# Adding the old attention state on TensorE, and updating the state earlier in the even groups

## The chip, the cores and the metric

The kernel runs on one core of a Trainium2 chip. The time is device microseconds (us) of one execution, from an uploaded program to the finished output; of the kernel before, the median of three runs is 358.19 us.

## The reference

Two stages follow each other. The first is a gated linear attention over 4 batches, 8 heads, 768 steps and 48 channels; the second a two-layer network on the 3072 resulting rows, with a rational function between its layers.

```python
f = 1.0 / (1.0 + np.exp(-f_logit))
for t in range(S):
    state = f[:, :, t, :, None] * state + einsum('bhd,bhe->bhde', k[:, :, t], v[:, :, t])
    y[:, :, t] = einsum('bhd,bhde->bhe', q[:, :, t], state)
...
h = x @ w_in                                   # 3072x384 by 384x2048
P = a[0] + a[1]*h + a[2]*h**2 + a[3]*h**3
Q = 1.0 + abs(b[0])*abs(h) + abs(b[1])*h**2
out = (P / (Q + 1e-6)) @ w_out                 # by 2048x384
```

## The kernel before

**Attention.** Time is cut into 6 chunks of 128 steps, the batches into 2 halves; a *unit* is one chunk of one half, so there are 12, numbered ku (chunk ku // 2, half ku % 2). Each half keeps its state in one SBUF tile `state`, 128 x 2 x 4 x 48 in bf16, for 2 batches and 4 head pairs. For a unit, ScalarE (ACT) takes exp and ln of the gates (`a_ef`), TensorE (PE) sums them along time (`a_cs`), ACT takes exp of the sums (`a_exp`: A and Ai), VectorE (DVE) scales q and k by them (`a_mul`), PE transposes the result (`a_T`) and ACT copies it (`a_Te`). PE forms the scores (`a_sc`), DVE masks them (`a_mask`: scm), and PE makes the output y from the old state and from the masked scores (`a_y`). ACT copies y (`a_ye`: ysb), PE transposes it (`a_x`: xps), and ACT copies that into xT (`a_xe`), the input of the network.

**The state.** `a_sv` (L147) puts two things into one PSUM bank `sv`: the column sums of the gates' logarithms (L156, 8 matmuls) and the chunk's increment of the state (L163, 16 matmuls). `a_al` (L213) has ACT turn the sums into the decay `alast`. `a_st` (L220) has DVE compute, in two instructions, stmp = sv + state (L232) and state = stmp * alast (L233); in chunk 0 there is no old state, and one product from `sv` does it (L229). The last chunk needs no update, so units 2 to 9 run the two instructions: eight times.

**One bank for two tiles.** `sv` and `xps` carry the tag w1 of the pool `ps1`, which has one buffer. So the transposes of `a_x` (L240) cannot start before the last reader of `sv` is done. That reader is L232 of the same unit.

**The network.** Its work is cut into 24 groups n: chunk c = n // 4 and a quarter g = n % 4 of the 2048 columns. PE multiplies (`m_h`, two halves into the one buffer `hp`), ACT copies (`m_y`: hy), DVE computes |h| and the denominator (`m_q`: z L280, w L282 and L283), ACT takes ln and exp(-ln) for the reciprocal (`m_ln`: lq L289, `m_ex`: qi L294), DVE computes the numerator (`m_p`: t, L301 to L305) and the product (`m_g`: gall L313). PE multiplies the finished chunk before by w_out (`m_o`, L330), ACT copies (`m_oe`, L340) and the SP queue writes it out.

**Order.** There is no scheduler: each engine runs its instructions in the order in which the program is written. The main loop (L435) takes a pair of groups at a time, p = 0 to 11, an *even* one and an *odd* one, and works the attention of unit ku = p + 3 in between. The even group finishes unit ku - 1 (y's copy, transposes, decay, state) and starts unit ku; the odd one continues unit ku up to y. In the even group the program writes `a_ye`, `m_h`, `a_x`, `a_exp`, `a_al`, `a_xe`, `m_ln`, `m_ex`, `m_p`, `m_o`, `m_y`, `m_h`, `a_mul`, `a_st`, `m_oe`, `a_T`, `m_g`. The eight state updates fall into the even groups of p = 0 to 7.

Loads of q, k and the gates go through the SP queue, those of v through GpSimd's (POOL), three units ahead. In the first 80 us GpSimd also casts the weights to bf16.

Of the kernel before, what the change touches and what calls it, by code (L numbers as in the profile page):

```python
# [8 lines left out]
F32 = mybir.dt.float32  # L9
# [8 lines left out]
def kernel(  # L18
# [12 lines left out]
    nc = tc.nc  # L31
    B, H, S, D = q.shape
    C = 128
    NC = S // C
    P = 128
    HP = H // 2
# [5 lines left out]
    UB = 2  # L42
# [11 lines left out]
    at = ctx.enter_context(tc.tile_pool(name="at", bufs=1))  # L54
# [12 lines left out]
    ident = consts.tile([C, C], BF16, name="ident")  # L67
    mask = consts.tile([C, C], F32, name="mask")
    ones = consts.tile([C, 1], BF16, name="ones")
# [47 lines left out]
    def a_exp(n):  # L117
        s = at_[n]
        s["A"] = at.tile([C, UB, H, D], F32, name="A")
        s["Ai"] = at.tile([C, UB, H, D], F32, name="Ai")  # L120
        for dst, sc in ((s["A"], -1.0), (s["Ai"], 1.0)):
            nc.scalar.activation(dst.rearrange("p b h d -> p b (h d)"), s["cs"][:, :, 0:DM],
                                 AF.Exp, scale=sc)
# [21 lines left out]
        s["qkT"] = t  # L145

    def a_sv(n):  # L147
        s = at_[n]
        if s["c"] == NC - 1:
            return  # L150
        sv = ps1.tile([P, 512], F32, name="sv", tag="w1")
        s["svv"] = sv[:, 0:UB * HP * D].rearrange("p (b h e) -> p b h e", b=UB, h=HP)
        s["al"] = sv[:, 448:448 + UB * HP]
        for j in range(UB):
            for p in range(HP):
                nc.tensor.matmul(s["al"][:, j * HP + p:j * HP + p + 1],  # L156
                                 s["ls"][:, j, 2 * p:2 * p + 2, :].rearrange("t h d -> t (h d)"),
                                 ones, start=True, stop=True)
        for j in range(UB):
            for p in range(HP):  # L160
                for i in range(2):
                    h = 2 * p + i
                    nc.tensor.matmul(s["svv"][64 * i:64 * i + 64, j, p, :],  # L163
                                     s["qk"][:, j, 1, h, :], s["vn"][:, j, h, :],
                                     start=True, stop=True)

    def a_sc(n, j):
        s = at_[n]
# [37 lines left out]
    def a_ye(n):  # L206
        s = at_[n]
        ysb = at.tile([C, UB, DM], BF16, name="ysb")
        nc.scalar.copy(ysb.rearrange("t b (p i e) -> t i (b p) e", p=HP, i=2),
                       s["y"].rearrange("t i b p e -> t i (b p) e"))  # L210
        s["ysb"] = ysb

    def a_al(n):  # L213
        s = at_[n]
        if s["c"] == NC - 1:
            return
        s["alast"] = at.tile([P, UB * HP], F32, name="alast")
        nc.scalar.activation(s["alast"], s["al"], AF.Exp, scale=-1.0)

    def a_st(n):  # L220
        s = at_[n]
        if s["c"] == NC - 1:
            return
        al = s["alast"]
        ab = bass.AP(tensor=al.tensor, offset=al.offset, ap=[al.ap[0], al.ap[1], [0, D]])
        stv = s["st"].rearrange("p b h e -> p (b h) e")
        svf = s["svv"].rearrange("p b h e -> p (b h) e")
        if s["c"] == 0:
            nc.vector.tensor_mul(stv, svf, ab)  # L229
        else:  # L230
            stmp = at.tile([P, UB * HP, D], F32, name="stmp")
            nc.vector.tensor_add(stmp, svf, stv)  # L232
            nc.vector.tensor_mul(stv, stmp, ab)  # L233

    def a_x(n):
        s = at_[n]
        xps = ps1.tile([P, UB, KD, C], BF16, name="xps", tag="w1")
        for j in range(UB):
            for kk in range(KD):
                nc.tensor.transpose(xps[:, j, kk, :], s["ysb"][:, j, kk * P:(kk + 1) * P], ident)  # L240
        s["xps"] = xps

    def a_xe(n):
        s = at_[n]
        c, u = s["c"], s["u"]
        if u == 0:
            xTs[c] = xp.tile([P, KD, B, C], BF16, name="xT")
        nc.scalar.copy(xTs[c][:, :, u * UB:(u + 1) * UB, :].rearrange("p k b t -> p b k t"), s["xps"])  # L248
# [5 lines left out]
    def m_h(n, half):  # L254
        if n >= NGR:
            return
        c, g = divmod(n, NG)
        hp = psh.tile([P, 2, NT], F32, name="hp", tag="h")
        xT = xTs[c].rearrange("p k b t -> p k (b t)")
        for e in range(2):  # L260
            m = g * G + half * 2 + e
            for kk in range(KD):
                nc.tensor.matmul(hp[:, e, :], w_in_sb[:, kk, m * P:(m + 1) * P], xT[:, kk, :],  # L263
                                 start=(kk == 0), stop=(kk == KD - 1))
        mg.setdefault(n, {})["hp", half] = hp

    def m_y(n, half):
        if n >= NGR:
            return
        s = mg[n]  # L270
        if half == 0:
            s["y"] = ms.tile([P, W], BF16, name="hy")
        nc.scalar.copy(s["y"][:, half * 2 * NT:(half + 1) * 2 * NT],  # L273
                       s["hp", half].rearrange("p a n -> p (a n)"))

    def m_q(n):

        s = mg[n]
        z = ms.tile([P, W], BF16, name="z", bufs=1)
        nc.vector.tensor_scalar(z.bitcast(U16), s["y"].bitcast(U16), 0x7FFF, None, op0=ALU.bitwise_and)  # L280
        w = ms.tile([P, W], BF16, name="w", bufs=1)
        nc.vector.tensor_scalar(w, z, babs[:, 1:2], babs[:, 0:1], op0=ALU.mult, op1=ALU.add)  # L282
        nc.vector.tensor_mul(w, w, z)  # L283
        s["w"] = w

    def m_ln(n):
        s = mg[n]
        s["lq"] = ms.tile([P, W], F32, name="lq", bufs=1)
        nc.scalar.activation(s["lq"], s["w"], AF.Ln, bias=one_eps)  # L289

    def m_ex(n):
        s = mg[n]
        s["qi"] = ms.tile([P, W], BF16, name="qi")
        nc.scalar.activation(s["qi"], s["lq"], AF.Exp, scale=-1.0)  # L294

    def m_p(n):

        s = mg[n]
        y = s["y"]
        t = ms.tile([P, W], BF16, name="t")  # L300
        nc.vector.tensor_scalar(t, y, a_sb[:, 3:4], a_sb[:, 2:3], op0=ALU.mult, op1=ALU.add)  # L301
        nc.vector.tensor_mul(t, t, y)  # L302
        nc.vector.tensor_scalar(t, t, a_sb[:, 1:2], None, op0=ALU.add)  # L303
        nc.vector.tensor_mul(t, t, y)  # L304
        nc.vector.tensor_scalar(t, t, a_sb[:, 0:1], None, op0=ALU.add)  # L305
        s["t"] = t
# [75 lines left out]
    a_sc(0, 0)  # L382
    a_sc(0, 1)
    a_sv(0)
    a_exp(1)
    a_mask(0, 0)
# [12 lines left out]
    a_sc(1, 0)  # L399
    a_sc(1, 1)  # L400
    a_sv(1)
    a_ef(2)
    a_mask(1, 0)
# [31 lines left out]
    for p in range(NGR // 2):  # L435
        ku = p + 3
        for odd in range(2):
            n = 2 * p + odd
            c, g = divmod(n, NG)
            last = c == NC - 1  # L440
            has, prev = ku < NUN, ku - 1 < NUN
            m_y(n + 1, 0)
            m_q(n)
            if not odd:
                if prev:
                    a_ye(ku - 1)
                m_h(n + 1, 1)
                if prev:
                    a_x(ku - 1)
                if has:  # L450
                    a_exp(ku)
                if prev:
                    a_al(ku - 1)
                    a_xe(ku - 1)
                m_ln(n)
                m_ex(n)
                m_p(n)
                m_o(c - 1, g)
                m_y(n + 1, 1)
                m_h(n + 2, 0)  # L460
                if has:
                    a_mul(ku)
                if prev:
                    a_st(ku - 1)
                m_oe(c - 1, g)
                if has:
                    a_T(ku)
            else:
                if has:
                    a_Te(ku)  # L470
                m_h(n + 1, 1)
                m_ln(n)
                m_ex(n)
                if has:
                    a_sc(ku, 0)
                    a_sc(ku, 1)
                    a_sv(ku)
                m_p(n)
                m_o(c - 1, g)
                m_y(n + 1, 1)  # L480
                m_h(n + 2, 0)
                if has:
                    a_mask(ku, 0)
                    a_mask(ku, 1)
                if ku + 1 < NUN:
                    a_ef(ku + 1)
                m_oe(c - 1, g)
                if has:
                    a_y(ku)
                if ku + 1 < NUN:  # L490
                    a_cs(ku + 1)
                if ku + 3 < NUN:
                    load(ku + 3)
            m_g(n)
            if last:
                for b in range(B):
                    m_o(c, b, range(g * G, (g + 1) * G))
# [32 lines left out]
```

## Time and profile before

| what | us |
|---|---|
| median of three runs (357.04 to 358.89) | 358.19 |
| the profiled execution, whole | 357.51 |
| its span, first to last instruction | 355.2 |
| busy in the span: DVE | 273.3 |
| busy in the span: ACT | 224.2 |
| busy in the span: PE | 206.3 |
| DVE idle ahead of gall (L313), 24 instances together | 39.8 |

An engine that works all the time would show 355.2 us of busy time. How the engines' idle times hang together is read from the waits and from the order of events in one pair. In the loop's middle a pair takes 27.8 us, from one even z to the next.

### The profile page before, as it was taken

What the parts mean: (1) busy time and instruction counts of PE and PEld (TensorE: products, weight loads), DVE (VectorE), ACT (ScalarE), POOL (GpSimd) and SP (SyncE); (2) the same over time, 40 slices, a digit from 0 to 9 for tenths busy, and PEclk for the clock granted to TensorE, in tenths of its full rate; (3) what the DMA queues carried; (4) which work ended last, traced back from release to release, by engine and by line L of the source; (5) the groups of instructions that cost most, each with busy time, mean ns of one, the idle gap of its engine ahead of it and who ended that gap; (6) DMA issues with size and microseconds to landing.
All of it is one profiled execution on the core that took longest, in us unless ns stands there. A gap on an engine that the chain in (4) does not pass through costs nothing.

```text
span 355.2 us, 4363 instructions
## 1 busy us (share of the span) xinstructions
PE 206.3 (58%) x1722; PEld 113.1 (32%) x1744; DVE 273.3 (77%) x290; ACT 224.2 (63%) x214; POOL 37.0 (10%) x42
## 2 busy tenths in 40 slices
PE   0364730750455881882683584575478575868764
PEld 0153320420223440441351352242244332334431
DVE  3264294998599499499499499499589999999981
ACT  4437545670683892793694586487389776776641
POOL 5032620460001001002002002000000000000000
PEclk9999995886586797697699699699699999699996
DMA  9998999698304009009109208300000000010002
GB/s 142 170 214 209 227 166 173 231 236 96 70 2 22 23 5 173 22 2 155 22 24 137 43 22 111 68 23 24 0 22 24 22 24 22 2 43 24 22 22 89
DMA packets 107315, 27.80 MB, mean 78 GB/s; under 512 B 100640, under 2 KB 105760, under 8 KB 107296
## 3 DMA queue, kind: packets, MB, share of 16 engines
q1 hardware_dynamic: 82336, 25.18, 34.0%
q0 software_dynamic: 24960, 2.36, 12.6%
q8 instruction: 13, 0.21, 0.3%
q14 instruction: 6, 0.05, 0.1%
HBM read 25.17 MB, written 4.72 MB: 84 GB/s over the span
## 4 chain that ended last, share of the span: by engine, by line
DVE 63%; ACT 15%; issue 7%; DMA 7%; PE 5%; SPq 2%; DVEq 0%; ACTq 0%
DVE gall L313 8%; DVE t L302 7%; DVE w L283 7%; DVE t L304 7%; DVE w L282 6%; ACT lq L289 5%; DMA kn<-in_k_dram 5%; DVE t L303 5%; DVE z L280 5%; ACT qi L294 4%; DVE scm L182 4%; DVE t L301 4%; DVE t L305 3%; DVE qkp L128 3%; DVE qkp L127 2%
## 5 line engine op out<-in xcount | busy, mean ns | idle before, releaser
L263 PE MATMUL hp<-xT,w_in_sb 128*128 128x512 bf16 x266 | 76.7, 412 | 53.1 <-ACT hy L273 50.0
L330 PE MATMUL op<-w_out_sb,gall 128*128 128x384 bf16 x384 | 80.1, 371 | 5.6 <-DVE gall L313 5.6
L273 ACT CAST hy<-hp 128x1024 bf16<-128x1024 f32 x48 | 48.1, 1003 | 26.2 <-PE hp L263 26.2
L313 DVE TENSOR_TENSOR gall<-t,qi 128x2048 bf16<-128x2048 bf16 x24 | 29.3, 1222 | 39.8 <-ACT qi L294 39.2
L263 PEld LDWEIGHTS <-w_in_sb 128*128 128x128 bf16 x288 | 29.7, 103 | 90.0 <-issue 68.0
L289 ACT ACTIVATE lq<-w,one_eps 128x2048 f32<-128x2048 bf16 x24 | 48.2, 2009 | 10.5 <-DVE w L283 10.5
L330 PEld LDWEIGHTS <-gall 128*128 128x128 bf16 x384 | 41.3, 111 | 39.6 <-issue 15.0
L248 ACT COPY xT<-xps 128x768 bf16<-128x768 bf16 x12 | 9.6, 803 | 67.2 <-PE xps L240 67.2
L294 ACT ACTIVATE qi<-lq 128x2048 bf16<-128x2048 f32 x24 | 45.8, 1910 | 0.8
L240 PE MATMUL xps<-ident,ysb 128*128 128x128 bf16 x72 | 9.1, 291 | 60.3 <-DVE stmp L232 60.1
L182 DVE TENSOR_TENSOR scm<-sc,mask 128x1024 bf16<-128x1024 f32 x24 | 28.2, 1217 | 16.4 <-PE sc L173 16.4
L97 POOL DMA_DIRECT2D vn<-in_v_dram x24 | 22.2, 930 | 133.9 <-PE y L193 133.1
L302 DVE TENSOR_TENSOR t<-t,hy 128x2048 bf16<-128x2048 bf16 x24 | 30.6, 1273 | 0.8
L304 DVE TENSOR_TENSOR t<-t,hy 128x2048 bf16<-128x2048 bf16 x24 | 29.4, 1226 | 0.8
L283 DVE TENSOR_TENSOR w<-w,z 128x2048 bf16<-128x2048 bf16 x24 | 29.4, 1225 | 0.8
L240 PEld LDWEIGHTS <-ysb 128*128 128x128 bf16 x72 | 7.1, 128 | 64.7 <-issue 62.3
L144 ACT COPY qkT<-tp 128x2048 bf16<-128x2048 bf16 x12 | 22.4, 1869 | 0.1
L282 DVE TENSOR_SCALAR w<-z,babs 128x2048 bf16<-128x2048 bf16 x24 | 20.9, 870 | 0.9
L303 DVE TENSOR_SCALAR t<-t,a_sb 128x2048 bf16<-128x2048 bf16 x24 | 19.3, 803 | 0.8
L136 PE MATMUL tp<-ident,qkp 128*128 128x128 bf16 x192 | 15.0, 237 | 7.8 <-DVE qkp L127 6.0
L301 DVE TENSOR_SCALAR t<-hy,a_sb 128x2048 bf16<-128x2048 bf16 x24 | 19.4, 807 | 0.0
L127 DVE TENSOR_TENSOR qkp<-qn,A 128x768 bf16<-128x768 f32 x12 | 11.4, 952 | 9.9 <-DMA qn<-in_q_dram 8.3
(45 smaller groups left out, 215.6 us busy)
## 6 DMA issues: line engine op xcount, KB each, us to landing
fn<-in_f_logit_dram SPq DMA_DIRECT2D x24, 192.0 KB, 5.4
kn<-in_k_dram SPq DMA_DIRECT2D x24, 192.0 KB, 6.2
qn<-in_q_dram SPq DMA_DIRECT2D x24, 192.0 KB, 4.8
out_dram<-osb SPq DMA_DIRECT2D x24, 192.0 KB, 1.9
wst<-in_moe_w_in_dram SPq DMA_DIRECT2D x4, 768.0 KB, 6.6
wst<-in_moe_w_out_dram SPq DMA_DIRECT2D x4, 768.0 KB, 6.0
vn<-in_v_dram POOLq DMA_DIRECT2D x24, 96.0 KB, 5.8
a_sb<-in_moe_a_dram SPq DMA_DIRECT2D x1, 2.0 KB, 3.9
```

Of the source, the lines that this page charges most:

```text
L182: nc.vector.tensor_mul(m, s["sc", j].rearrange("s i p t -> s (i p) t"), mb)
L263: nc.tensor.matmul(hp[:, e, :], w_in_sb[:, kk, m * P:(m + 1) * P], xT[:, kk, :], start=(kk == 0), stop=(kk == KD - 1))
L273: nc.scalar.copy(s["y"][:, half * 2 * NT:(half + 1) * 2 * NT], s["hp", half].rearrange("p a n -> p (a n)"))
L282: nc.vector.tensor_scalar(w, z, babs[:, 1:2], babs[:, 0:1], op0=ALU.mult, op1=ALU.add)
L283: nc.vector.tensor_mul(w, w, z)
L289: nc.scalar.activation(s["lq"], s["w"], AF.Ln, bias=one_eps)
L294: nc.scalar.activation(s["qi"], s["lq"], AF.Exp, scale=-1.0)
L302: nc.vector.tensor_mul(t, t, y)
L303: nc.vector.tensor_scalar(t, t, a_sb[:, 1:2], None, op0=ALU.add)
L304: nc.vector.tensor_mul(t, t, y)
L313: nc.vector.tensor_mul(galls[c][:, g * G:(g + 1) * G, :].rearrange("p a n -> p (a n)"), s["t"], s["qi"])
L330: nc.tensor.matmul(ops[c, b], galls[c][:, mm, b * C:(b + 1) * C], w_out_sb[:, mm, :], start=(mm == 0), stop=(mm == KF - 1))
```

## The change

`a_sv` now adds the old state on PE: between the column sums and the increment one matmul, with the identity as weights and the state as moving operand, goes into the columns of the increment, and the 16 increment matmuls accumulate on it. Only the first of the column sums starts the bank afresh. `a_st` is then a single product from `sv`, in every chunk. In the even groups `a_al` and `a_st` are written ahead of `a_ye`.

```diff
     def a_sv(n):
...
+        s["svf"] = sv[:, 0:UB * HP * D]
+        svv = s["svf"].rearrange("p (b h e) -> p b h e", b=UB, h=HP)
...
-                                 ones, start=True, stop=True)
+                                 ones, start=(j + p == 0), stop=True, skip_group_check=True)
+        if s["c"] > 0:
+            nc.tensor.matmul(s["svf"], ident, s["st"].rearrange("p b h e -> p (b h e)"),
+                             start=False, stop=True, skip_group_check=True)
...
-                    nc.tensor.matmul(s["svv"][64 * i:64 * i + 64, j, p, :],
+                    nc.tensor.matmul(svv[64 * i:64 * i + 64, j, p, :],
                                      s["qk"][:, j, 1, h, :], s["vn"][:, j, h, :],
-                                     start=True, stop=True)
+                                     start=False, stop=True, skip_group_check=True)
...
     def a_st(n):
...
-        stv = s["st"].rearrange("p b h e -> p (b h) e")
-        svf = s["svv"].rearrange("p b h e -> p (b h) e")
-        if s["c"] == 0:
-            nc.vector.tensor_mul(stv, svf, ab)
-        else:
-            stmp = at.tile([P, UB * HP, D], F32, name="stmp")
-            nc.vector.tensor_add(stmp, svf, stv)
-            nc.vector.tensor_mul(stv, stmp, ab)
+        nc.vector.tensor_mul(s["st"].rearrange("p b h e -> p (b h) e"),
+                             s["svf"].rearrange("p (x e) -> p x e", e=D), ab)
...
             if not odd:
                 if prev:
+                    a_al(ku - 1)
+                    a_st(ku - 1)
                     a_ye(ku - 1)
...
                 if prev:
-                    a_al(ku - 1)
                     a_xe(ku - 1)
...
-                if prev:
-                    a_st(ku - 1)
```

DVE in the even group of one pair, before (in brackets the semaphores that an instruction waits for, by engine):

```order
L282 TENSOR_SCALAR w<-z,babs 128x2048 [waits DVE_49]
L283 TENSOR_TENSOR w<-w,z 128x2048 [waits DVE_49]
L301 TENSOR_SCALAR t<-hy,a_sb 128x2048
L302 TENSOR_TENSOR t<-t,hy 128x2048 [waits DVE_49]
L303 TENSOR_SCALAR t<-t,a_sb 128x2048 [waits DVE_49]
L304 TENSOR_TENSOR t<-t,hy 128x2048 [waits DVE_49]
L305 TENSOR_SCALAR t<-t,a_sb 128x2048 [waits DVE_49]
L127 TENSOR_TENSOR qkp_103<-qn,A 128x2x8x48 [waits DMAHW1_49,DMAHW0_49,Activation_49]
L128 TENSOR_TENSOR qkp_103<-kn,Ai 128x2x8x48 [waits DMAHW7_49,DMAHW6_49,Activation_49]
L232 TENSOR_TENSOR stmp<-sv,state_106 128x384 [waits PE_49,Activation_49]
L233 TENSOR_TENSOR state_106<-stmp,alast 128x384 [waits DVE_49,PE_49]
L313 TENSOR_TENSOR gall<-t,qi 128x2048 [waits Activation_49]
```

The same engine and place now (the line numbers are those of the changed kernel):

```order
L281 TENSOR_SCALAR w<-z,babs 128x2048 [waits DVE_49]
L282 TENSOR_TENSOR w<-w,z 128x2048 [waits DVE_49]
L231 TENSOR_TENSOR state_107<-sv,alast 128x384 [waits PE_49,Activation_49]
L300 TENSOR_SCALAR t<-hy,a_sb 128x2048
L301 TENSOR_TENSOR t<-t,hy 128x2048 [waits DVE_49]
L302 TENSOR_SCALAR t<-t,a_sb 128x2048 [waits DVE_49]
L303 TENSOR_TENSOR t<-t,hy 128x2048 [waits DVE_49]
L304 TENSOR_SCALAR t<-t,a_sb 128x2048 [waits DVE_49]
L127 TENSOR_TENSOR qkp_102<-qn,A 128x2x8x48 [waits DMAHW1_49,DMAHW0_49,Activation_49]
L128 TENSOR_TENSOR qkp_102<-kn,Ai 128x2x8x48 [waits DMAHW7_49,DMAHW6_49,Activation_49]
L312 TENSOR_TENSOR gall<-t,qi 128x2048 [waits DVE_49,Activation_49]
```

The last reader of `sv` stood behind five instructions of the numerator and two of `a_mul`; it stands right behind w now, and the addition is gone.

ACT in the same group, before (from the copy of the next group's h to the reciprocal):

```order
L273 CAST hy<-hp 128x1024 [waits DVE_49,PE_49]
L209 CAST ysb<-y 128x2x8x48 [waits PE_49]
L122 ACTIVATE A<-cs 128x768 [waits PE_49]
L122 ACTIVATE Ai<-cs 128x768
L218 ACTIVATE alast<-sv 128x8
L248 COPY xT<-xps 128x2x3x128 [waits PE_49]
L289 ACTIVATE lq<-w,one_eps 128x2048 [waits DVE_49]
```

And now:

```order
L272 CAST hy<-hp 128x1024 [waits DVE_49,PE_49]
L223 ACTIVATE alast<-sv 128x8
L214 CAST ysb<-y 128x2x8x48 [waits PE_49]
L122 ACTIVATE A<-cs 128x768 [waits PE_49]
L122 ACTIVATE Ai<-cs 128x768
L247 COPY xT<-xps 128x2x3x128 [waits PE_49]
L288 ACTIVATE lq<-w,one_eps 128x2048 [waits DVE_49]
```

The decay moved from behind y's copy and two exponentials to ahead of them; xT and the reciprocal keep their places.

## Rows read from the trace of the kernel before

**Rows 1.** The waits: engine, line <- releaser: us together, times, longest

```profile
PE xps L240 <- DVE stmp L232: 60.1, 8, 8.9
PE hp L263 <- ACT hy L273: 50.0, 39, 5.6
...
DVE gall L313 <- ACT qi L294: 39.2, 8, 4.9
```

**Rows 2.** Timeline, DVE, even group of p = 5: start, duration, work [idle before]

```profile
187.91 0.69 DVE L280 TENSOR_SCALAR z<-hy 128x2048 uint16<-128x2048 uint16 x1
188.64 1.12 DVE L282 TENSOR_SCALAR w<-z,babs 128x2048 bf16<-128x2048 bf16 x1
...
190.94 0.81 DVE L301 TENSOR_SCALAR t<-hy,a_sb 128x2048 bf16<-128x2048 bf16 x1
...
195.76 0.95 DVE L127 TENSOR_TENSOR qkp<-qn,A 128x768 bf16<-128x768 f32 x1
...
197.50 0.55 DVE L232 TENSOR_TENSOR stmp<-sv,state 128x384 f32<-128x384 f32 x1
198.15 0.56 DVE L233 TENSOR_TENSOR state<-stmp,alast 128x384 bf16<-128x384 f32 x1
203.61 1.23 DVE L313 TENSOR_TENSOR gall<-t,qi 128x2048 bf16<-128x2048 bf16 x1 [4.90 <-ACT qi L294]
204.75 0.69 DVE L280 TENSOR_SCALAR z<-hy 128x2048 uint16<-128x2048 uint16 x1
```

**Rows 3.** Timeline, ACT, the same group

```profile
190.64 0.21 ACT L218 ACTIVATE alast<-sv 128x8 f32<-128x8 f32 x1
198.94 0.80 ACT L248 COPY xT<-xps 128x768 bf16<-128x768 bf16 x1 [8.08 <-PE xps L240]
199.63 2.00 ACT L289 ACTIVATE lq<-w,one_eps 128x2048 f32<-128x2048 bf16 x1
201.67 1.91 ACT L294 ACTIVATE qi<-lq 128x2048 bf16<-128x2048 f32 x1
```

**Rows 4.** Timeline, PE, the same group

```profile
187.52 0.58 PE L193 MATMUL y<-vn,scm 128*128 128x48 bf16 x16
...
198.10 0.80 PE L240 MATMUL xps<-ident,ysb 128*128 128x128 bf16 x6 [7.92 <-DVE stmp L232]
```

**Rows 5.** Groups by line: busy us, mean ns | idle us before

```profile
L113 PE MATMUL cs<-lsp,U 128*128 128x384 bf16 x24 | 7.1, 384 | 7.5 <-ACT lsp L107 7.5
...
L233 DVE TENSOR_TENSOR state<-stmp,alast 128x384 bf16<-128x384 f32 x8 | 4.5, 558 | 0.8
L232 DVE TENSOR_TENSOR stmp<-sv,state 128x384 f32<-128x384 f32 x8 | 4.4, 552 | 0.0
...
L229 DVE TENSOR_TENSOR state<-sv,alast 128x384 bf16<-128x384 f32 x2 | 1.1, 546 | 0.0
```

**Rows 6.** Windows, pairs p = 5 and p = 8: length, PE, PEld, DVE, ACT, POOL busy, clock, DMA

```profile
187.91:215.68 27.77, 16.78 (x158) 9.27 (x156) 22.35 (x25) 18.43 (x19) 1.84 (x2) 0.88 0.42 65
...
270.90:292.30 21.40, 15.02 (x138) 8.33 (x136) 20.98 (x24) 18.29 (x17) 0.00 (x0) 1.00 0.08 28
```

**Rows 7.** Timeline, DVE, even group of p = 8, which has no state update

```profile
270.90 0.69 DVE L280 TENSOR_SCALAR z<-hy 128x2048 uint16<-128x2048 uint16 x1
...
280.17 1.22 DVE L313 TENSOR_TENSOR gall<-t,qi 128x2048 bf16<-128x2048 bf16 x1
```

**Rows 8.** Timeline, ACT, the same group

```profile
276.40 1.91 ACT L294 ACTIVATE qi<-lq 128x2048 bf16<-128x2048 f32 x1
```

**Rows 9.** Timeline, DVE, first instruction of p = 1

```profile
75.97 1.96 DVE L280 TENSOR_SCALAR z<-hy 128x2048 uint16<-128x2048 uint16 x1
```

**Rows 10.** Timeline, POOL: the last of four casts of w_out

```profile
75.78 1.61 POOL L352 CAST w_out_sb<-wst 128x1536 bf16<-128x1536 f32 x1 [1.79 <-DMA wst<-in_moe_w_out_dram]
```

**Rows 11.** Timeline, SP queue: the last loads of unit 4

```profile
49.40 3.52 SPq L97 DMA_DIRECT2D qn<-in_q_dram  x2
```

**Rows 12.** Timeline, PE, p = 2: the first product with w_out

```profile
115.38 5.14 PE L330 MATMUL op<-w_out_sb,gall 128*128 128x384 bf16 x16
```

More of the change, by code (lines that the diff above doesn't have):

```diff
@@ L151, in a_sv @@
         sv = ps1.tile([P, 512], F32, name="sv", tag="w1")
-        s["svv"] = sv[:, 0:UB * HP * D].rearrange("p (b h e) -> p b h e", b=UB, h=HP)
+        s["svf"] = sv[:, 0:UB * HP * D]
+        svv = s["svf"].rearrange("p (b h e) -> p b h e", b=UB, h=HP)
         s["al"] = sv[:, 448:448 + UB * HP]
```

## The prediction

> **What bounds the kernel now.** I read the waits first, then one pair of groups on DVE, ACT and PE in order of time, then the windows by pair, and last a pair without a state update.
>
> The waits show three large ones [rows 1]. PE waits eight times, 60.1 us together, for stmp before it may transpose y. DVE waits eight times, 39.2 us together, for qi before gall. PE's 50.0 us ahead of hp are spread over 39 waits, no instance over 5.6. Eight is the number of state updates, so the first two belong to the even groups of p = 0 to 7.
>
> One even group shows that they are one chain [rows 2 to 4]. DVE runs z and w, the numerator t, `a_mul`, and only then stmp, from 197.50 to 198.05. PE, idle for 7.92 us, starts xps at 198.10; ACT, idle for 8.08 us, copies xT at 198.94, then runs lq and qi, which ends at 201.67 + 1.91 = 203.58. Behind state DVE has only gall left, which needs qi: it stands for 4.90 us and starts at 203.61. So DVE, late with stmp, makes itself wait. Every pair has this: 8 x 4.90 = 39.2.
>
> Outside that hole DVE is the bound. In the pair of p = 5 it is busy for 22.35 us of 27.77, ACT for 18.43, PE for 16.78 [rows 6]. In the pair of p = 8, where no state is updated and xps waits for nothing on DVE, the pair takes 21.40 us with DVE busy for 20.98 [rows 6]: DVE never stands there, and qi is ready at 276.40 + 1.91 = 278.31, 1.86 us before gall at 280.17 [rows 7, 8]. That is nearly the state in which the change would put p = 0 to 7.
>
> **The change, part by part.**
>
> *The addition goes from DVE.* Eight stmp of 552 ns are 4.4 us, and the idle 0.8 us between stmp and state goes with them [rows 5]: 5.2 us, all on DVE, which is the bound.
>
> *The remaining product reads PSUM instead of SBUF.* Before, the product of chunks 1 to 4 reads stmp in SBUF and takes 558 ns; the one of chunk 0 is exactly the new instruction, from `sv`, and takes 546 ns [rows 5]. I take no change. [...]
>
> *The identity matmul comes to PE.* A matmul of 128x384 takes 384 ns in the mean of cs, its nearest relative [rows 5]: 8 x 0.384 = 3.1 us. It stands in the odd group ahead of `m_o`; behind `m_o` comes hp, which waits for ACT's hy anyway [rows 1]. I take 0; without that cover 3.1 us, and below zero nothing, since it only adds work. Its operand state is written a chunk earlier, so it waits for nothing.
>
> *The state update moves ahead of the numerator.* The old place of state cost DVE the 39.2 us. In the new place I count from z of the even group. DVE reaches state after z and w: 190.94 - 187.91 = 3.03 us. What state needs is there: y's last matmul, which reads the old state, ends at 188.10, 2.84 us ahead [rows 4]; alast, at 190.64 before, no longer stands behind y's copy and the two exponentials. State takes 0.55 and ends at 3.58. From the end of stmp to xT took 198.94 - 198.05 = 0.89 us, from xT to the end of qi 203.58 - 198.94 = 4.64 us [rows 2, 3]. So qi ends at 3.58 + 0.89 + 4.64 = 9.11. Meanwhile DVE runs the numerator, 195.76 - 190.94 = 4.82, and `a_mul`, 197.50 - 195.76 = 1.74, and comes to gall at 3.58 + 6.56 = 10.14. qi is 1.03 us early, the wait is gone: 39.2 us. What is queued behind state on DVE if it should wait is t, `a_mul` and gall. What was behind xps on PE and xT on ACT all comes earlier, too: the odd group starts 10.14 + 1.14 - 9.11 = 2.17 us after qi, before 204.75 - 203.58 = 1.17, so ACT has a microsecond more in hand there than now.
>
> *alast ahead of ysb* delays ysb and the exponentials by its 0.21 us [rows 3]. All of them stand ahead of xT, which waits for state until 3.58 + 0.89; 0.
>
> *DVE back to back.* The end of state and the start of the next instruction overlap a little where nothing waits (L127's duration is 0.95, its step less); at most 0.08 us for each, 0.2 us in all taken.
>
> *Loads.* No load is moved in the code, but the buffers come free earlier and the data are wanted earlier. In p = 1 `a_mul` of unit 4 comes some 6 us sooner, at about 79; the last load of unit 4 has left the SP queue at 49.40 + 3.52 = 52.92 [rows 11]. The last cast of w_out ends at 77.39 [rows 10], and its first user, at 115.38 before [rows 12], moves to no earlier than 115.38 - 3 x 5.6 = 98.6. 0.
>
> *Casts against DVE.* z of p = 1 takes 1.96 us instead of 0.69, right over a cast of GpSimd [rows 2, 9, 10]: 1.27 us. There are four such casts in p = 0 and 1, and other DVE instructions will meet them now. None hit or all four hit is 0 to 5.1 us, an estimate from that one row; three of the four are overlapped by such a delay in the trace of before, so the change lies between 3.8 us less and 1.3 us more. I take none.
>
> **Sum.** 39.2 + 5.2 + 0.2 = 44.6 us. The profiled execution took 357.51 us (its span 355.2 and 2.31 around it), so 357.51 - 44.6 = 312.9 us. It lies 0.7 us under the median of the runs shown, from which the same sum gives 313.6; I take the middle, 313.2. A pair would take 27.77 - 5.57 = 22.2 us.
>
> **The rivals.**
>
> *A rest of the wait stays before gall.* The margin of qi is 1.03 us, less than the 1.86 of p = 8. If alast, y or xps come 2 us later than I lay out, DVE stands for 1 us in each pair: 8 us, 321. For it speaks that state, xps, xT, lq and qi are still a chain in a row over three engines; against it that y and alast are over 2 us early by the rows.
>
> *The first two pairs give nothing.* There the loads and casts still run, and PE has no `m_o`. If they are bound by arriving data, 2 x 5.57 = 11.1 us are lost: 324. Against it: z of p = 1 waits for nothing [rows 9], and the loads of unit 4 have left 26 us before they would be used.
>
> *It doesn't do what it says.* If xps still waited for something as late as stmp did, only the addition would go: 357.5 - 5.2 = 352. Against it: the order on DVE shows state behind w, and no other late reader of `sv`.
>
> [...]
>
> **How the numbers follow.** The forecast has 0.75, the rest of the wait 0.12, the first two pairs 0.07, the change that does nothing but save the addition 0.03, PE as the bound 0.02, and 0.01 is left for what I don't see. The range reaches down by the casts, 312.9 - 3.8 = 309.1, and up over the first rival and most of the second, to 322. Faster by over 0.5% (1.8 us, about what a measurement of this kernel can tell from no change) is all but the last: 0.96; within 0.5% 0.02; slower 0.02.
>
> **What the new profile would show.** Right: the waits of xps for state below 2.5 us each, or gone from the top of the list; no wait of gall for qi; state at 546 ns; DVE nearly without idle time from p = 0 to p = 11, a pair at 22.2 us; the clock near 1.00 from p = 2 on. Wrong: waits of gall for qi, of state for alast or y, or of z for hy; waits of `a_mul` for loads in p = 1; a clock that is lower than before in the middle pairs.

## The result and the profile after

The changed kernel takes 312.08 us in the median of four runs (310.16 to 312.86), before 358.17 (357.04 to 358.89). The ratio is 0.872, 95% interval 0.867 to 0.876: 46.1 us faster. The forecast was 313.2 us, in a range of 309 to 322. The profiled execution took 310.16 us, its span is 307.8 (before 357.51 and 355.2).

Where [rows 1] had 60.1 us of PE waiting for stmp and 39.2 us of DVE waiting for qi, the waits of the changed kernel read (engine, line <- releaser: us together, times, longest):

```profile
PE hp L262 <- ACT hy L272: 57.7, 33, 5.6
...
ACT xT L247 <- PE xps L239: 14.7, 10, 3.8
...
PE xps L239 <- DVE state L231: 10.8, 8, 2.2
```

All of DVE's own waits, the same view:

```profile
DVE scm L187 <- PE sc L178: 16.4, 3, 6.9
DVE qkp L127 <- DMA qn<-in_q_dram: 8.2, 1, 8.2
DVE osb L337 <- ACT osb L339: 2.1, 1, 2.1
DVE osb L337 <- DMA out_dram<-osb: 2.0, 1, 2.0
DVE qkp L127 <- ACT A L122: 1.7, 1, 1.7
DVE lsp L358 <- PEq L512: 0.9, 1, 0.9
DVE qkp L359 <- issue: 0.3, 2, 0.2
```

gall no longer stands in the list. What is left belongs to the prologue (scm, qkp, lsp) and to the last two outputs (osb). The even group of p = 5 on DVE, beside [rows 2] (start, duration, work):

```profile
159.18 0.68 DVE L279 TENSOR_SCALAR z<-hy 128x2048 uint16<-128x2048 uint16 x1
159.90 1.05 DVE L281 TENSOR_SCALAR w<-z,babs 128x2048 bf16<-128x2048 bf16 x1
...
162.12 0.55 DVE L231 TENSOR_TENSOR state<-sv,alast 128x384 bf16<-128x384 f32 x1
162.59 0.80 DVE L300 TENSOR_SCALAR t<-hy,a_sb 128x2048 bf16<-128x2048 bf16 x1
...
167.40 0.95 DVE L127 TENSOR_TENSOR qkp<-qn,A 128x768 bf16<-128x768 f32 x1
...
169.14 1.22 DVE L312 TENSOR_TENSOR gall<-t,qi 128x2048 bf16<-128x2048 bf16 x1
170.28 0.69 DVE L279 TENSOR_SCALAR z<-hy 128x2048 uint16<-128x2048 uint16 x1
```

From z to z it takes 11.10 us, before 16.84. The same group on ACT and on PE, beside [rows 3, 4]:

```profile
159.75 0.19 ACT L223 ACTIVATE alast<-sv 128x8 f32<-128x8 f32 x1
...
163.25 0.80 ACT L247 COPY xT<-xps 128x768 bf16<-128x768 bf16 x1 [1.22 <-PE xps L239]
...
165.99 1.91 ACT L293 ACTIVATE qi<-lq 128x2048 bf16<-128x2048 f32 x1
...
171.60 1.01 ACT L272 CAST hy<-hp 128x1024 bf16<-128x1024 f32 x1 [2.42 <-PE hp L262]
```

```profile
162.72 0.49 PE L239 MATMUL xps<-ident,ysb 128*128 128x128 bf16 x6 [1.36 <-DVE state L231]
163.06 2.76 PE L329 MATMUL op<-w_out_sb,gall 128*128 128x384 bf16 x16
168.85 2.72 PE L262 MATMUL hp<-xT,w_in_sb 128*128 128x512 bf16 x6 [3.03 <-ACT hy L272]
...
172.67 1.46 PE L262 MATMUL hp<-xT,w_in_sb 128*128 128x512 bf16 x6
...
175.31 0.32 PE L162 MATMUL sv<-state,ident 128*128 128x384 bf16 x1
```

xps still starts as soon as the bank is free, 0.05 us behind the state's end at 162.67, but that is 3.54 us behind z, before 10.19. qi ends at 165.99 + 1.91 = 167.90, 1.24 us ahead of gall. The new instructions as groups by line (busy us, mean ns | idle before), beside [rows 5]:

```profile
L231 DVE TENSOR_TENSOR state<-sv,alast 128x384 bf16<-128x384 f32 x10 | 5.5, 549 | 0.0
...
L162 PE MATMUL sv<-state,ident 128*128 128x384 bf16 x8 | 2.6, 322 | 0.0
```

The windows of the first two pairs and of p = 5 (length, PE, PEld, DVE, ACT, POOL busy, clock, DMA), beside [rows 6]:

```profile
46.24:69.21 22.97, 12.07 (x107) 6.08 (x109) 22.55 (x24) 16.99 (x15) 5.01 (x4) 0.78 1.19 202
69.21:93.37 24.16, 12.58 (x137) 6.38 (x131) 23.74 (x25) 17.98 (x17) 4.84 (x4) 0.79 0.93 153
...
159.18:181.21 22.03, 16.25 (x150) 8.66 (x147) 21.61 (x25) 18.29 (x19) 1.84 (x2) 0.92 0.54 81
```

Laid side by side from first z to first z, in us:

| stretch | before | after | difference |
|---|---|---|---|
| p = 0 and 1 | 58.52 | 47.13 | 11.39 |
| p = 2 to 7 | 166.08 | 131.44 | 34.64 |
| p = 8 to the last z | 65.70 | 65.69 | 0.01 |
| ahead of the first z, and behind the last | 64.9 | 63.5 | 1.4 |

So the whole gain of the profiled executions but 1.4 us lies in the eight pairs with a state update, 5.75 us for each in the mean.

### The profile page after: what moved, and what is told of

Read it like the earlier page. It is cut to its first block, busy times and chain, and to the rows that moved or that the text cites. A ratio compares the mean times of both kernels' runs of the same rounds, so it can differ in the third digit from the quotient of the medians.

```text
span 307.8 us, 4394 instructions
## 1 busy us (share of the span) xinstructions
PE 202.7 (66%) x1752; PEld 110.9 (36%) x1752; DVE 267.3 (87%) x282; ACT 224.6 (73%) x214; POOL 36.4 (12%) x42
## 4 chain that ended last, share of the span: by engine, by line
DVE 63%; issue 11%; DMA 9%; PE 6%; ACT 5%; SPq 5%; DVEq 0%; ACTq 0%
DVE gall L312 9%; DVE t L303 7%; DVE t L301 7%; DVE w L281 6%; DVE w L282 6%; SPq L97 5%; DVE scm L187 5%; DVE t L300 5%; DVE t L302 4%; DVE z L279 4%; DMA qn<-in_q_dram 4%; DVE qkp L128 3%; DVE t L304 3%; PE op L329 3%; DMA fn<-in_f_logit_dram 2%
## 5 line engine op out<-in xcount | busy, mean ns | idle before, releaser
L262 PE MATMUL hp<-xT,w_in_sb 128*128 128x512 bf16 x288 | 84.1, 435 | 59.3 <-ACT hy L272 57.7
L272 ACT CAST hy<-hp 128x1024 bf16<-128x1024 f32 x48 | 48.2, 1004 | 33.4 <-PE hp L262 33.4
L329 PE MATMUL op<-w_out_sb,gall 128*128 128x384 bf16 x384 | 67.9, 332 | 3.9 <-DVE gall L312 3.9
L288 ACT ACTIVATE lq<-w,one_eps 128x2048 f32<-128x2048 bf16 x24 | 48.2, 2007 | 8.2 <-DVE w L282 8.1
L329 PEld LDWEIGHTS <-gall 128*128 128x128 bf16 x384 | 36.9, 99 | 29.6 <-DVE gall L312 5.3
L293 ACT ACTIVATE qi<-lq 128x2048 bf16<-128x2048 f32 x24 | 45.9, 1911 | 0.8
L282 DVE TENSOR_TENSOR w<-w,z 128x2048 bf16<-128x2048 bf16 x24 | 30.7, 1279 | 0.8
L312 DVE TENSOR_TENSOR gall<-t,qi 128x2048 bf16<-128x2048 bf16 x24 | 30.4, 1268 | 0.7
L303 DVE TENSOR_TENSOR t<-t,hy 128x2048 bf16<-128x2048 bf16 x24 | 29.4, 1226 | 0.8
L301 DVE TENSOR_TENSOR t<-t,hy 128x2048 bf16<-128x2048 bf16 x24 | 29.4, 1225 | 0.8
L136 PE MATMUL tp<-ident,qkp 128*128 128x128 bf16 x192 | 18.2, 265 | 7.9 <-DVE qkp L127 6.1
L136 PEld LDWEIGHTS <-qkp 128*128 128x128 bf16 x192 | 16.6, 124 | 14.1 <-DVE qkp L127 6.9
L300 DVE TENSOR_SCALAR t<-hy,a_sb 128x2048 bf16<-128x2048 bf16 x24 | 20.4, 851 | 0.0
L304 DVE TENSOR_SCALAR t<-t,a_sb 128x2048 bf16<-128x2048 bf16 x24 | 18.1, 754 | 0.8
L302 DVE TENSOR_SCALAR t<-t,a_sb 128x2048 bf16<-128x2048 bf16 x24 | 18.1, 753 | 0.8
```

What stands on the lines that cost most here:

```text
L312: nc.vector.tensor_mul(galls[c][:, g * G:(g + 1) * G, :].rearrange("p a n -> p (a n)"), s["t"], s["qi"])
L329: nc.tensor.matmul(ops[c, b], galls[c][:, mm, b * C:(b + 1) * C], w_out_sb[:, mm, :], start=(mm == 0), stop=(mm == KF - 1))
```

## The experiments

All runs stand beside runs of the kernel before on the same chip; their medians were 357.5 to 358.9 us. The changed kernel, run again with the last group, took 311.34 us (309.76 to 312.23).

> The changed kernel as it is, beside the two others on the same chip, as their measure: 312 us (311 to 313).

**The move alone.** The kernel before, with decay and update at the new place; DVE still adds.

```diff
                 if prev:
+                    a_al(ku - 1)
+                    a_st(ku - 1)
                     a_ye(ku - 1)
...
-                    a_al(ku - 1)
                     a_xe(ku - 1)
...
-                if prev:
-                    a_st(ku - 1)
```

> Only the move: decay and state update stand ahead of y's copy in the even groups, and VectorE still adds the old state in stmp. My theory: the gain has two parts that add up, 39.2 us from the eight waits of 4.90 us ahead of gall and 5.2 us from the eight additions. stmp releases the bank at the same place as the new product does, so this kernel keeps the first part and loses the second: 312.1 + 5.2 = 317.3 us (316 to 319), and no wait of gall for qi. Rival: the matmul is what frees the bank, and the move is worth little without it: 350 or more.

Measured: 316.63 us (316.55 to 317.45), ratio 0.887 (0.883 to 0.892). gall waits nowhere, and PE's wait for the bank is nearly as short as with the whole change (10.8 us there):

```profile
PE xps L240 <- DVE stmp L232: 12.4, 8, 2.6
```

So the move alone brings 41 us. It is 4.6 to 5.3 us longer than the changed kernel (by that kernel's two medians, 312.08 and 311.34): the additions.

**The identity matmul alone.** The changed kernel, with decay and update at their old places.

```diff
                 if prev:
-                    a_al(ku - 1)
-                    a_st(ku - 1)
                     a_ye(ku - 1)
...
+                    a_al(ku - 1)
                     a_xe(ku - 1)
...
                     a_mul(ku)
+                if prev:
+                    a_st(ku - 1)
```

> Only the identity matmul: the old state is added on TensorE, the single product stands in the old place behind the scaling of q and k. My theory: the chain xps, xT, lq, qi starts when the last reader of the bank ends. Before that was stmp, at 197.50 to 198.05 in the middle pair; now the product takes that place and ends at the same time. VectorE then waits 4.90 + 0.65 = 5.55 us ahead of gall, and the 5.2 us of additions turn into waiting: 358.2 us, within 1 us. Rival (the one in the prediction that let the addition alone go, 352): VectorE's work sets the time, so less work gives 358.2 - 5.2 = 353.

Measured: 357.11 us, ratio 1.0005 (0.9975 to 1.0035): no change. Its waits:

```profile
PE xps L239 <- DVE state L231: 60.6, 8, 8.3
...
DVE gall L312 <- ACT qi L293: 44.5, 8, 5.6
```

DVE does 5.2 us less and waits 44.5 - 39.2 = 5.3 us more [rows 1]. The bank's last reader starts the chain, and at the old place the single product ends where stmp ended (10.13 us behind z in p = 5, before 10.14), so the chain starts no earlier. What was taken from the work of DVE comes back as its wait.

**How late the update may stand.** The changed kernel, with the update behind the first or the second instruction of the numerator (the diff is that of the first).

```diff
-    def m_p(n):
+    def m_p(n, mid=None):
...
         nc.vector.tensor_scalar(t, y, a_sb[:, 3:4], a_sb[:, 2:3], op0=ALU.mult, op1=ALU.add)
+        if mid:                    # one instruction later
+            mid()
         nc.vector.tensor_mul(t, t, y)
...
                     a_al(ku - 1)
-                    a_st(ku - 1)
                     a_ye(ku - 1)
...
-                m_p(n)
+                m_p(n, (lambda: a_st(ku - 1)) if prev else None)
```

> The changed kernel with the state update one instruction later, behind the first of the numerator (0.84 us later on VectorE). My theory: qi is 1.24 us early in the changed kernel, and 1.24 is more than 0.84, so no wait of gall for qi appears and the time stays: 312 us, within 1.5 us. Rival: the two instructions of the run before cost 6 us because each step behind w costs its own length, so one step costs 8 x 0.84 x 0.4 = 2.7 us or more: 315.

> The changed kernel with the state update two instructions later, behind the first two of the numerator (0.84 + 1.26 = 2.10 us later on VectorE). My theory: qi is 1.24 us early in the changed kernel's middle pairs (167.90 against gall at 169.14), so a wait of 2.10 - 1.24 = 0.86 us comes back in each of eight pairs: 312.1 + 6.9 = 319 us (316 to 321), with a wait of gall for qi of about 0.9 us eight times. Rival: any place ahead of the scaling of q and k is early enough, since ScalarE was idle for xT anyway: 312.

Measured: one later 310.48 us, ratio 0.867 (0.865 to 0.870), as the changed kernel; two later 318.0 us, ratio 0.891 (0.887 to 0.895). ACT of the first, in a middle pair, and gall there:

```profile
164.61 0.80 ACT L247 COPY xT<-xps 128x768 bf16<-128x768 bf16 x1 [0.33 <-PE xps L239]
...
167.34 1.91 ACT L293 ACTIVATE qi<-lq 128x2048 bf16<-128x2048 f32 x1
```

```profile
169.65 1.22 DVE L314 TENSOR_TENSOR gall<-t,qi 128x2048 bf16<-128x2048 bf16 x1
```

qi ends at 169.25 and gall starts at 169.65, without waiting: 0.40 us of the margin are left. Two later, one row of a pair and the waits:

```profile
173.89 1.23 DVE L314 TENSOR_TENSOR gall<-t,qi 128x2048 bf16<-128x2048 bf16 x1 [1.12 <-ACT qi L293]
```

```profile
DVE gall L314 <- ACT qi L293: 6.3, 7, 1.1
```

6.3 us of waits, and the time is 6 to 7 us longer. So the edge lies between 0.84 and 2.10 us, as the margin of 1.24 us says. That the shared bank is the link is read from the waits and from these runs, which move its last reader; no run gives xps a bank of its own.

**The decay in its old place.** The changed kernel, with alast behind the exponentials on ACT; on DVE nothing moves.

```diff
                 if prev:
-                    a_al(ku - 1)
-                    a_st(ku - 1)
                     a_ye(ku - 1)
...
+                    a_al(ku - 1)
+                    a_st(ku - 1)
                     a_xe(ku - 1)
```

> The changed kernel with the decay alast back in its old place on ScalarE, behind y's copy and the two exponentials; the state update keeps its new place on VectorE. My theory: that part of the move is worth little. In the changed kernel's middle pairs alast would end at about 162.1, and VectorE comes to the state at 162.12 (161.9 in pairs without a load of v beside w): a wait of state for alast of 0 to 0.3 us a pair, 0 to 2 us in all, 312 to 314 us. Rival: the decay had to move too, since the state then waits for it behind the copies, a microsecond or more a pair: 320 or more.

Measured: 313.35 us, ratio 0.873 (0.870 to 0.875), 2.0 us above the changed kernel beside it. The time is as expected, the reason is another. DVE waits for alast once, for 0.3 us. But z and w of a middle pair take 1.98 us together:

```profile
159.98 1.05 DVE L279 TENSOR_SCALAR z<-hy 128x2048 uint16<-128x2048 uint16 x1
161.07 0.93 DVE L281 TENSOR_SCALAR w<-z,babs 128x2048 bf16<-128x2048 bf16 x1
```

GpSimd issues the loads of v beside them, by the estimate in the last section. In the pair of the changed kernel shown above z and w take 0.68 and 1.05, together 1.73 us. I had not counted on this. In p = 2 to 7 of one execution of each, z and w of the even groups make up 1.3 of the 1.7 us by which this kernel is longer than the changed one beside it; no run tests it apart.

**More work on PE.** The changed kernel with 8, and with 32, more identity matmuls a unit, which the column sums then overwrite.

```diff
         s["al"] = sv[:, 448:448 + UB * HP]
+        if s["c"] > 0:
+            for _ in range(8):     # or 32
+                nc.tensor.matmul(s["svf"], ident, s["st"].rearrange("p b h e -> p (b h e)"),
+                                 start=True, stop=True, skip_group_check=True)
```

> The changed kernel with eight more identity matmuls of 128x384 in each of units 2 to 9, ahead of the column sums and overwritten by them. My theory: the added matmul costs nothing, since TensorE waits for hy behind it; eight more take about 8 x 0.17 = 1.4 us a pair in the odd group, of which 0.6 lie in that wait, and the rest delays hy by 0.8 us where ScalarE still has over 1 us in hand ahead of xT: 312 us, within 1.5 us. Rival: TensorE's work lies on the path, 8 x 1.4 = 11 us more: 323.

> The changed kernel with 32 instead of 8 more identity matmuls in each of units 2 to 9, 32 x 0.164 = 5.2 us a pair by the run with eight. My theory: the cover of TensorE's work ends where hy of the next group comes after alast is needed. hp would end 3.9 us later than with eight, hy at 3.0 us behind z, alast at 3.9, so the state waits about 1.3 us a pair on VectorE: 8 x 1.3 = 10 us, 322 us (318 to 327). Rival that the cover has no such end, or TensorE has more room than that: 312; rival that TensorE is the bound with each matmul counting: 8 x 5.2 = 42 us more, 354.

Measured: with 8 more 311.47 us, ratio 0.871 (0.868 to 0.875), nothing; with 32 more 327.78 us, ratio 0.915 (0.911 to 0.919), above the range of 318 to 327. PE in the odd group of p = 5 with 8 more:

```profile
173.78 1.47 PE L158 MATMUL sv<-state,ident 128*128 128x384 bf16 x8
...
178.53 1.46 PE L266 MATMUL hp<-xT,w_in_sb 128*128 128x512 bf16 x5
```

The eight take 1.47 us, and DVE waits for state in no pair: alast ends 2.69 us ahead of state in the next even group, and 1.21 in that of p = 4, the least of p = 2 to 7. That hp follows its predecessor without a wait is not their doing alone, for PE also came to this group earlier than in the changed kernel: the hp ahead of the scores took 1.46 us and not 2.72. With 32 more, ACT and DVE in the even group of p = 5:

```profile
172.29 0.48 ACT L343 COPY osb<-op 128x384 f32<-128x384 f32 x1 [3.09 <-PE op L333]
173.58 1.01 ACT L276 CAST hy<-hp 128x1024 bf16<-128x1024 f32 x1 [0.82 <-PE hp L266]
174.49 0.18 ACT L227 ACTIVATE alast<-sv 128x8 f32<-128x8 f32 x1
```

```profile
174.71 0.56 DVE L235 TENSOR_TENSOR state<-sv,alast 128x384 bf16<-128x384 f32 x1 [3.04 <-PE cs L113]
```

The place is the one expected: DVE waits ahead of state in six of the eight pairs, 15.4 us together, and alast ends at 174.67, 0.04 us before state here. (The row names cs, which ended last on PE; what releases state is alast.) The size is not: 3.04 us in this pair, not 1.3. One pair later hp, in the odd group of p = 5, and state, in the even group of p = 6:

```profile
182.26 1.46 PE L266 MATMUL hp<-xT,w_in_sb 128*128 128x512 bf16 x6 [3.22 <-ACT hy L276]
```

```profile
198.41 0.56 DVE L235 TENSOR_TENSOR state<-sv,alast 128x384 bf16<-128x384 f32 x1 [1.77 <-PE cs L113]
```

My count missed two things. I had added the 3.9 us once. The late xT also delays hy, which ends 0.70 us ahead of the odd group's z and not 1.19 as in the run with 8 more, so PE starts its longer piece 0.5 us later against z, too: the delay comes round. And I had counted from a pair in which hp takes 1.46 us. Ahead of the 3.04 us, in the odd group of p = 4, it was later: ACT, with hy, waited 2.43 us for it there, and 1.16 one pair later.

```profile
160.06 1.01 ACT L276 CAST hy<-hp 128x1024 bf16<-128x1024 f32 x1 [2.43 <-PE hp L266]
...
183.75 1.01 ACT L276 CAST hy<-hp 128x1024 bf16<-128x1024 f32 x1 [1.16 <-PE hp L266]
```

That is 1.27 us more, and the wait of state is 1.27 us longer, 3.04 against 1.77. The granted clock was 0.7 in the slice of the page from 154 to 162 us, and 0.9 in that from 178 to 187.

**Is DVE the bound now?** The changed kernel, with the first step of the numerator of the odd groups on ACT, where it waits 2.42 us for hp; then also that of the three last even groups.

```diff
+    def m_t(n):
+        s = mg[n]
+        s["t"] = ms.tile([P, W], BF16, name="t")
+        nc.scalar.activation(s["t"], s["y"], AF.Identity, scale=a_sb[:, 3:4], bias=a_sb[:, 2:3])
...
                 m_oe(c - 1, g)                          # even group
+                m_t(n + 1)
                 if has:
                     a_T(ku)
...
                 m_oe(c - 1, g)                          # odd group, second kernel only
+                if ku + 1 >= NUN and n + 1 < NGR:
+                    m_t(n + 1)
```

(`m_p` then begins with the product by y.)

> The changed kernel with the first step of the numerator (t = a3 y + a2) of the twelve odd groups computed on ScalarE, in the even group behind the output's copy, where it waits 2.42 us for hp. My theory: VectorE is the bound from the first pair to the last and ScalarE has the room, so each pair gets shorter by the step's 0.84 us: 12 x 0.84 = 10 us, 302 us (300 to 305). Rival: the chain over ScalarE is nearly as long as VectorE's work, and the 1.9 us more on ScalarE delay hy, alast or qi: waits on VectorE of a microsecond a pair come back and the time is 312 or more.

> The run before this one, and also the first step of the three even groups of the last three pairs on ScalarE, where no attention is left. My theory: VectorE is the bound there too, 3 x 0.84 = 2.5 us less than that run: 299.5 us. Rival: in these groups ScalarE waits for w and VectorE for qi in turn, so what is taken from VectorE there comes back as a wait for qi: the same time as that run.

Measured: 301.59 us, ratio 0.843 (0.840 to 0.845), and 301.53 us, ratio 0.843 (0.840 to 0.846). The first does what DVE as the bound says (12 x 0.84 = 10.1 us): 9.8 to 10.5 us less, middle pairs of 20.95 us. A window of one:

```profile
153.97:174.92 20.95, 16.06 (x151) 9.24 (x152) 20.56 (x24) 20.14 (x20) 1.75 (x2) 0.92 0.57 86
```

DVE and ACT are now nearly even, 20.56 and 20.14 us of 20.95. The step costs ACT 2.10 us in the same execution; on DVE it takes 0.85, in the mean of the changed kernel (L300):

```profile
163.65 2.10 ACT L298 ACTIVATE t<-hy,a_sb 128x2048 bf16<-128x2048 bf16 x1
```

The second brought nothing that the runs can tell, as its rival said for the first of the three groups:

```profile
248.65 1.23 DVE L320 TENSOR_TENSOR gall<-t,qi 128x2048 bf16<-128x2048 bf16 x1 [2.74 <-ACT qi L293]
```

There the 2.1 us on ACT delay hy, ysb, xT and with them qi. In the other two groups the wait is 0 and 0.47 us; from the first z of p = 9 to the last z this kernel is 0.4 us shorter than the one before it, by one execution of each.

## Why the prediction was right, point by point

**The eight waits, 39.2 us.** Right. Not one is left, and the move alone brings 41 us.

**The additions, 5.2 us.** Right in the sum, 4.6 to 5.3 by the run that keeps them. But they do not stand for themselves, as the sum has them: without the move they bring 0. My third rival counted on 352 us for a change that only takes the addition away; the run says 357. What was wrong there is the price of work taken from a bound engine at a place where its end starts the chain that the engine waits for.

**The product from PSUM, 0.** Right: 549 ns over its ten instances, 558 from SBUF [rows 5].

**The identity matmul, 0.** Right, and more than that: nine of them cost nothing, 33 cost 16 us.

**The margin ahead of gall, 1.03 us.** It is 1.24. From the state's end to xT took 163.25 - 162.67 = 0.58 us, not 0.89: xps takes 0.49 us instead of 0.80 [rows 4], at a granted clock of 1.00 during its six matmuls, before 0.50. The runs with a later update put the edge where the margin says.

**alast ahead of ysb.** I took 0 for it as a cost, and it is; as a help it was worth next to nothing in waiting (0.3 us once).

**DVE back to back, 0.2 us.** Too small. The next instruction starts 0.47 us behind the start of state (162.12 to 162.59); before, DVE waited for qi behind state, and all its 0.56 us counted. That is 0.09 us a pair, 0.7 in eight.

**The loads, 0.** Right: `a_mul` of unit 4 starts at 79.56 and waits for nothing. The first product with w_out starts at 97.01, earlier than the 98.6 that I gave as its bound, because `m_o` moves ahead within its own pair, too; the last cast of w_out had ended at 75.00.

**The casts, 0 between -3.8 and +1.3.** In the profiled execution three instructions met a cast, as before: gall at 66.90 took 2.39 us, w at 70.78 2.50 and the first t at 73.67 1.88. p = 0 and 1 together became 11.39 us shorter, 2 x 5.57 = 11.14 were counted. In the executions of the changed kernel and of the runs with one instruction later, with 8 more matmuls and with the late decay they took 45.9 to 48.2 us, so to about a microsecond it is luck that this came out near 0.

**The first two pairs (second rival).** They gave all that was counted; no load is waited for there.

**The sum.** 44.6 us were counted, 46.1 measured between the medians, 47.4 between the profiled executions. Of these 2.8 us more, 0.2 are in p = 0 and 1. 1.2 lie in p = 2 to 7 (34.64 against 6 x 5.57): about 0.4 from state back to back, and 0.6 from z and w of the even groups, which take 9.6 us instead of 10.2 beside the loads that GpSimd issues. The last 1.4 lie outside the pairs, mostly behind the last z: the last 16 products with w_out take 2.77 us there, before 4.37, at granted clocks of 1.00 and 0.62. One row of each kernel:

```profile
345.60 4.37 PE L330 MATMUL op<-w_out_sb,gall 128*128 128x384 bf16 x16 [3.49 <-DVE gall L313]
```

```profile
299.51 2.77 PE L329 MATMUL op<-w_out_sb,gall 128*128 128x384 bf16 x16 [1.81 <-DVE gall L312]
```

That is luck of these executions, not the change: in the run with 8 more matmuls, whose program is the same there, the stretch from the last z to the end of the span takes 18.6 us again (290.37 to 309.0), as before (336.60 to 355.2), and not 17.3 (290.50 to 307.8).

**The clock near 1.00.** Wrong, without a price. Five of the six pairs p = 2 to 7 show 0.92, that of p = 6 1.00. In the pair of p = 5, behind 3.03 us of waiting for hy, six matmuls of hp take 2.72 us at a granted clock of 0.50 (168.8 to 171.6); the next six of hp take 1.46, and in p = 6 the first six take 1.46, too, behind the same wait of 3.03 us. What decides between the two is not shown. The pair of p = 5 is 0.24 us longer than that of p = 6, and w alone is that much longer in it, 1.05 against 0.81 us: the clock costs nothing there, since hp lies beside DVE's work. With 32 more matmuls, where the page shows 0.7, hp comes later and that does cost, 1.27 us ahead of state, as shown above.

**PE as the bound (chance 0.02).** It did not come: the clock rose from 0.88 to 0.92 in the pair of p = 5. The work of that pair before and the identity matmul, 16.78 + 0.38 = 17.2 us [rows 5, 6], taken as work at full clock, would fill 27.77 us at a mean clock of 17.2 / 27.77 = 0.62, an estimate; no pair of p = 2 to 7 of the changed kernel shows less than 0.92. By work, PE had 22.03 - 16.25 = 5.8 us to spare in that pair. But spare time is not the measure: with 5.2 us more ahead of `m_o` the pairs are longer through the order of the work, over osb, hy and alast.

## What to carry to other kernels

When an engine that is busy most of the time waits at a fixed place, look for what it does itself, earlier in its own order, that starts the chain it waits for, and move that ahead; its place counts, not its length. Work taken from a bound engine in front of such a wait gains nothing until the wait is gone: the addition alone left the time here at 357.11 us. How far a step may slide can be read from the trace, as the time from the chain's end to its use, and a kernel on either side of that edge shows it.

## What the runs showed of the hardware that was not expected

DVE instructions can be longer beside the loads of v that GpSimd issues, and in the two kernels it goes with when the issue begins. In their even groups of p = 2 to 7, w, which starts 0.72 us behind z, took 1.05 to 1.22 us where the issue began 0.40 to 0.57 us behind z, and 0.81 where it began 0.64 us behind or later, or not at all, also where it then ran beside w. z took 0.68 to 0.69 us in all of them; with the late decay it took 1.05 to 1.06 in p = 3, 4 and 5, and with the move alone 1.06 in p = 3. In p = 5 of the late decay the issue lies about 0.3 us ahead of z, an estimate: in both kernels the issue began 0.29 to 0.31 us behind the end of y, for which it waits, and there y ends at 158.99 + 0.37 = 159.36 and z starts at 159.98. Two pairs of the changed kernel, p = 2 and p = 5 (w of the second, of 1.05 us, is shown above at 159.90):

```profile
94.09 0.81 DVE L281 TENSOR_SCALAR w<-z,babs 128x2048 bf16<-128x2048 bf16 x1
```

```profile
94.30 1.96 POOL L97 DMA_DIRECT2D vn<-in_v_dram  x2 [17.39 <-PE y L198]
...
159.58 1.84 POOL L97 DMA_DIRECT2D vn<-in_v_dram  x2 [20.19 <-PE y L198]
```

So a change that moves nothing on DVE itself may cost some time here by shifting what stands beside what. The first z of p = 0 stood between 44.9 and 47.8 us in the executions that were profiled, whatever the kernel, while the prologue's loads arrived; two kernels that differ by 2 us can't be told apart by single runs.
